# A fused attention and feed-forward kernel: 120 instead of 112 blocks of exponentials shared with VectorE

## The chip, the cores and the metric

The kernel runs on one core of a Trainium2 chip. TensorE (PE) multiplies matrices into PSUM, ScalarE (ACT) takes exponentials and other functions, VectorE (DVE) does elementwise work, GpSimd (POOL) small side work, and SyncE (SP) issues DMAs. The metric is device time in microseconds, the median of several runs. Before the change it is 861.0 us (three runs, 860.99 to 861.55).

## The reference

The input `A_x` has 2048 rows of 640. It is normalised; one branch is attention with 32 heads of 20, the other a feed-forward mixer, and the result joins them:

```python
xn = layernorm(x)                                   # 2048 x 640
q, k, v = split(xn @ wqkv)                          # 32 heads of 20
p = softmax(q @ k.T * 20 ** -0.5)                   # 32 x 2048 x 2048
s = concat(p @ v) @ wo
h = gelu(layernorm(xn) @ w1)                        # then four column groups shifted by rows
x1 = xn + shifted(h) @ w2
b = x1 + gelu(layernorm(x1) @ w3) @ w4              # inner width 1536
out = x + s * silu(b)
```

The attention has 32 x 2048 x 2048 = 134 million exponentials, by far the most of the elementwise work.

## The kernel before

**Tiling.** Heads are taken in 8 *quads* of 4. For each quad the queries are taken in 4 *groups* of 512, so there are 32 groups, written quad.group here and run one after the other (`attn_quad`, line 1184). In a group the 2048 keys are 16 *key tiles* of 128. For one key tile and four heads the scores are 128 x 2048; a *half* is two heads, 128 x 1024, and fills two PSUM banks.

**A plain key tile** (`score_act`, line 1378): TensorE computes the scores of each half either by rows (line 1375: four-row-group matmuls, the four heads at once) or by columns (line 1390); ScalarE takes one exponential of each half from PSUM to SBUF (`exp_act`, line 1432); then TensorE adds the weighted sum with the values, four matmuls at once (line 1233), into one PSUM bank that holds the group's output. Some key tiles score both halves in one step by rows, and a few take both halves in one wide exponential of 128 x 2048 (`score_rows`, lines 1398 to 1418). Which positions do so stands in the table `NR` (line 501): a number is a position in the group's list of plain tiles, 100 added means wide. Positions beyond the list have no effect.

**A shared block** (`score_both`, line 1438, and `block_bits`, line 1341) covers two key tiles. TensorE scores each of them by rows, all four heads in one step. ScalarE takes the exponential of one half of each tile. VectorE takes the other half: it turns the scores into 16-bit integers by one multiply and add out of PSUM (line 1459), which read as bfloat16 are a straight-line approximation of the exponential; three more copies with a constant added (line 1358) give the approximation at other offsets, and TensorE sums all four against weighted values (line 1367), so that the mean of the four is close to the exponential. For two of the four the values carry a factor, and these scaled values are made once by GpSimd (line 1179) for the key tiles 2, 3, 6, 7, 10, 11, 14, 15 that blocks use (`BLK`). The copies run over one block (2048 wide, a *single*) or over two (4096 wide, a *pair*). So a block has two exponentials on ScalarE where two plain tiles have four, and five weighted sums where two plain tiles have two.

**How many blocks a group has** is in the table `ND` (line 510), by quad and group, 0 to 4. `order` (line 520) builds the group's list of steps from it: with n blocks, 16 - 2n plain tiles are left, and `UNITS` (line 488) says at which positions the blocks stand, one block as a single, two as a pair, three as a pair and a single, four as two pairs. The last group of the last quad is built apart (`last_half`, line 1245) with two shared key tiles of its own. The table counts 112 blocks; its last entry, 4, is not used by that group, so 108 are run.

**Beside the attention** run, spread over the groups: the first normalisation, projections of values (first in group 0.0, then in quad 1) and of queries and keys for later heads (`stack`), the feed-forward branch (first layers in quads 0 and 1, normalisation and third and fourth layers in quads 2 to 6, with long Gelu instructions on ScalarE), and in the last quad the output projection, with the gate on VectorE. All of their matmuls go into three single PSUM banks (4, 5, 6) and are taken out mostly by VectorE.

**Buffers.** Seven PSUM banks serve scores and the other matmuls: a plain half takes banks 0, 1 or 2, 3; a shared tile takes one of these pairs and two of the banks 4, 5, 6, or both pairs. Where the two banks are not neighbours (4 and 6) VectorE's conversion is two instructions of 512. There are seven SBUF buffers for exponentials (`PT`), two for a pair's integers (`U`) and three for copies (`SS`).

**What sets the order.** No engine chooses anything at run time. `TABLE` (line 1812) is a long string; two characters name a task, and one more the PSUM banks or buffer that it gets. `follow` (line 217) reads it from left to right, and each engine's queue has its tasks in that order. `plan_sync` (line 304) then derives the semaphore waits from reads, writes and the reuse of buffers. Each queue is strictly in order, so a waiting instruction holds back all behind it on its engine.

**After a group** (`normalise`, line 1466) VectorE transposes the output in 32 x 32 blocks out of PSUM, takes the reciprocals of the sums, multiplies, transposes back, and SP stores the heads with four DMAs. Each group but 0.0 also loads a copy of its queries with four DMAs.

Of the kernel before, what the change touches and what calls it, by code (L numbers as in the profile page):

```python
# [453 lines left out]
class Cfg:  # L454
# [5 lines left out]
    def __init__(self, S=2048, D=640, H=32, F=1536):  # L460
# [50 lines left out]
            [0, 4, 4, 3],  # L511
            [4, 4, 4, 4],
            [3, 1, 4, 4],
            [4, 3, 4, 4],
            [3, 4, 4, 4],
            [4, 3, 4, 4],
            [3, 4, 4, 4],
            [4, 3, 2, 4])
# [56 lines left out]
class Gen:  # L575
# [29 lines left out]
    def A(self, name, *key):  # L605
        a = (name,) + key
        self.pl.own(name, a)
        return a
# [1324 lines left out]
```

## Time and profile before

| | us |
|---|---|
| median of three runs | 861.0 |
| the profiled execution's own time | 861.55 |
| its span, first to last instruction | 859.6 |
| ScalarE busy | 815.5 |
| PE busy | 800.6 |
| VectorE busy | 734.7 |
| 788 exponentials of 128 x 1024 (line 1432), busy | 733.1 |
| conversions on VectorE (line 1459), busy | 263.7 |
| shifted copies (line 1358), busy | 194.7 |

A profile line of a group reads: kernel line, engine, operation, output and input names, shapes, count, then the time in which the group was busy, the mean length of one in ns, the idle time of the engine just before its instructions and what ended most of that. Instructions of one engine overlap by a little, so the sum of lengths is above the time that they take. Matmuls are pipelined four at a time and their ends are modelled, so that a PE shown as busy may still take more work.

### The profile page before, as it was taken

How to read it: one execution, taken by the hardware profiler on the slowest of the kernel's cores; microseconds unless marked ns; L12 is line 12 of the kernel's file. 1: busy time of each engine (PE TensorE's matmuls, PEld its weight loads, DVE VectorE, ACT ScalarE, POOL GpSimd, SP SyncE). 2: the span in 40 equal slices, each digit the busy share in tenths (PEclk: the TensorE clock that was granted, in tenths of full speed). 3: DMA queues.
4: the chain of work that ended last, by engine and by line, in shares of the span. 5: the costliest groups of instructions: out<-in, count | busy, mean ns of one | idle time of the engine just before them, and what ended most of it. 6: DMA issues, size and time to landing. Idle time of an engine off the chain costs nothing.

```text
span 859.6 us, 31925 instructions
## 1 busy us (share of the span) xinstructions
PE 800.6 (93%) x14542; PEld 338.8 (39%) x14542; DVE 734.7 (85%) x1031; ACT 815.5 (95%) x854; POOL 39.3 (5%) x75
## 2 busy tenths in 40 slices
PE   7999999999899999999988999999997899989996
PEld 4443333334344433333433444343333343424464
DVE  7649999998998899999877999998995889987655
ACT  7799999999999999999999999999999999999994
POOL 5510000000000000000000000000000000000000
PEclk9999999999999999999999999999999999999998
DMA  7000533222110022311033011313211102041312
GB/s 230 18 16 24 137 97 89 90 66 65 25 40 16 18 50 55 79 44 46 11 94 92 14 51 27 81 36 89 50 32 47 34 13 54 13 123 33 116 57 95
DMA packets 74487, 50.83 MB, mean 59 GB/s; under 512 B 44768, under 2 KB 69552, under 8 KB 74352
## 3 DMA queue, kind: packets, MB, share of 16 engines
q1 hardware_dynamic: 74352, 48.79, 21.1%
q8 instruction: 115, 1.88, 0.9%
q14 instruction: 20, 0.16, 0.1%
HBM read 34.53 MB, written 10.17 MB: 52 GB/s over the span
## 4 chain that ended last, share of the span: by engine, by line
ACT 63%; PE 29%; DVE 7%; issue 1%; DMA 1%; SPq 0%; DVEq 0%
ACT arena L1432 57%; PE psum L640 10%; PE psum L1375 5%; PE psum L1390 4%; PE psum L1367 3%; PE psum L1233 3%; DVE arena L1459 2%; ACT arena L1787 2%; PE psum L1274 1%; ACT arena L1803 1%; DVE arena L1358 1%; ACT arena L1414 1%; ACT arena L1716 1%; DVE arena L852 1%; PE psum L963 1%
## 5 line engine op out<-in xcount | busy, mean ns | idle before, releaser
L1432 ACT ACTIVATE arena<-psum 128x1024 bf16<-128x1024 f32 x788 | 733.1, 1039 | 20.8 <-PE psum L1375 17.8
L640 PE MATMUL psum<-arena 128*32 128x320 bf16 (+1 forms) x5952 | 359.2, 335 | 0.6 <-DVE arena L1459 0.2
L1459 DVE TENSOR_SCALAR arena<-psum 128x1024 uint16<-128x1024 f32 (+1 forms) x243 | 263.7, 1094 | 31.8 <-PE psum L1375 30.5
L640 PEld LDWEIGHTS psum<-arena 128*32 128x32 bf16 x5952 | 148.8, 97 | 132.6 <-issue 31.2
L1375 PE MATMUL psum<-arena 32*128 32x512 bf16 x1384 | 165.6, 387 | 34.6 <-ACT arena L1432 24.2
L1358 DVE TENSOR_SCALAR arena<-arena 128x4096 uint16<-128x4096 uint16 (+1 forms) x174 | 194.7, 1142 | 2.9 <-PE psum L1367 1.8
L1390 PE MATMUL psum<-arena 128*32 128x512 bf16 x2400 | 182.7, 381 | 3.1 <-ACT arena L1432 2.1
L1233 PE MATMUL psum<-arena 128*22 128x512 bf16 x1552 | 148.9, 383 | 2.4 <-ACT arena L1432 2.0
L1367 PE MATMUL psum<-arena 128*22 128x512 bf16 x1728 | 146.2, 381 | 3.3 <-DVE arena L1358 3.1
L1375 PEld LDWEIGHTS psum<-arena 32*128 32x128 bf16 x1384 | 42.0, 91 | 179.5 <-ACT arena L1432 115.1
L1390 PEld LDWEIGHTS psum<-arena 128*32 128x32 bf16 x2400 | 46.1, 95 | 69.3 <-ACT arena L1432 57.7
L1367 PEld LDWEIGHTS psum<-arena 128*22 128x22 bf16 x1728 | 40.6, 91 | 53.6 <-issue 15.5
L1233 PEld LDWEIGHTS psum<-arena 128*22 128x22 bf16 x1552 | 38.8, 91 | 49.9 <-issue 18.6
L1109 DVE CAST arena<-psum 128x512 bf16<-128x512 f32 x40 | 27.0, 682 | 11.7 <-PE psum L640 11.4
L1783 DVE CAST arena<-psum 128x512 bf16<-128x512 f32 x48 | 32.7, 681 | 3.0 <-PE psum L640 2.5
L1567 DVE SCALAR_TENSOR_TENSOR arena<-psum,arena 128x320 bf16<-128x320 f32 x32 | 15.5, 489 | 22.5 <-PE psum L640 22.3
L1171 DVE CAST arena<-psum 128x320 bf16<-128x320 f32 x32 | 15.1, 486 | 16.2 <-PE psum L640 16.0
L852 DVE BATCH_NORM_STATS2 arena<-arena 128x6 f32<-128x320 bf16 x54 | 23.7, 477 | 3.2 <-DMA arena<-in_A_x_dram 3.1
L1480 DVE STREAM_TRANSPOSE arena<-psum 128x512 f32<-128x512 f32 x31 | 21.9, 708 | 1.7 <-PE psum L1367 1.2
L1490 DVE STREAM_TRANSPOSE arena<-arena 128x512 bf16<-128x512 bf16 x31 | 21.8, 702 | 0.2
L1744 DVE TENSOR_TENSOR arena<-psum,arena 128x320 bf16<-128x320 f32 x32 | 15.1, 480 | 7.2 <-PE psum L640 7.0
L1488 DVE TENSOR_TENSOR arena<-arena 128x512 bf16<-128x512 f32 x31 | 21.1, 680 | 0.1
(118 smaller groups left out, 364.2 us busy)
## 6 DMA issues: line engine op xcount, KB each, us to landing
arena<-in_B_w_dram SPq DMA_DIRECT2D x48, 160.0 KB, 2.6
arena<-arena SPq DMA_DIRECT2D x124, 32.0 KB, 2.2
arena<-in_B_w_dram SPq DMA_DIRECT2D x4, 960.0 KB, 5.7
arena<-in_A_x_dram SPq DMA_DIRECT2D x8, 320.0 KB, 5.9
arena<-in_A_x_dram SPq DMA_DIRECT2D x16, 160.0 KB, 2.3
out_dram<-arena SPq DMA_DIRECT2D x16, 160.0 KB, 1.8
heads<-arena SPq DMA_DIRECT2D x112, 20.0 KB
arena<-keys SPq DMA_DIRECT2D x28, 80.0 KB
```

The lines of the kernel that those rows point to most:

```text
L640: ins = e.matmul(pb[32 * c:32 * c + 32, 0:N], lhsT(k, c), rhs(k, c), start=(k == 0), stop=(stop and k == nk - 1), tile_position=(0, 32 * c))
L852: lambda e, li=li, n=n, hh=hh: e.bn_stats(st[:, li, 6 * hh:6 * hh + 6], xn[:, n, hD * hh:hD * hh + hD]),
L1109: T("dve", c_dve(512), lambda e, h=h, c=c: e.tensor_copy(KS[:, 512 * c:512 * c + 512], self.wbank(h)[:, 0:512]), reads=[wa], writes=[A("KS ...
L1233: ins = e.matmul(pb[32 * i:32 * i + 22, 0:512], VA[:, ql, kts[i // 2], i, :], PT[:, slots[i // 2][0].slot, 512 * (i % 2):512 * (i % 2) + 512],
L1358: T("dve", c_dve(w, "4x"), lambda e, v=v, dst=dst: e.tensor_scalar(dst, U[:, ub, 0:w], EXP_B[v], None, op0=ALU.add), reads=halves, writes= ...
L1367: ins = e.matmul(pb[32 * i:32 * i + 22, 0:512], wv, dst[:, at:at + 512].bitcast(BF16), start=first, stop=final, tile_position=(0, 32 * i))
L1375: return e.matmul(out, self.KT[32 * i:32 * i + 32, b, 128 * kt:128 * kt + 128], self.QT[32 * i:32 * i + 32, b, 512 * qc:512 * qc + 512], s ...
L1390: ins = e.matmul(out[32 * c:32 * c + 32, :], self.KT[:, b, 128 * kt + 32 * c:128 * kt + 32 * c + 32], self.QM[:, gb, 2 * a + jj, :], start ...
L1432: lambda e: e.activation(self.PT[:, hp.slot, :], self.psum[:, 512 * hs.slot:512 * hs.slot + 1024], AF.Exp, scale=cfg.scale),
L1459: ins = e.tensor_scalar(U[:, ub, 1024 * at + 512 * k:1024 * at + 512 * k + w], self.psum[:, 512 * hd.slots[k]:512 * hd.slots[k] + w], a_ex ...
L1480: T("dve", c_dve(512), lambda e: e.transpose(Ob[:, :], self.bank(self.PVB)[:, :]), writes=[("PV", 0), A("Ob")], name=f"ob{quad}_{qc}", cls ...
L1783: T("dve", c_dve(512), lambda e, h=h, fc=fc, i=i: e.tensor_copy(GT[:, i, fc, :], self.wbank(h)[:, 0:512]), reads=[wa], writes=at, name=f"g ...
```

## The change

Two things change: six entries of `ND`, and `TABLE`, whose every line differs. Quad 0 group 0 goes from 0 to 2 blocks, quad 2 group 1 from 1 to 3, quad 4 group 0 and quad 6 group 0 from 3 to 4, quad 7 group 1 from 3 to 4 and quad 7 group 2 from 2 to 3. The table counts 120 blocks, of which 116 are run. `NR`, `UNITS`, the buffers and all functions stay; because the list of plain tiles gets shorter, an entry of `NR` beyond its end loses its effect (a wide exponential at position 9 of quad 7 group 1, a row-scored tile at position 8 of quad 6 group 0).

```diff
         self.ND = (
-            [0, 4, 4, 3],
+            [2, 4, 4, 3],
             [4, 4, 4, 4],
-            [3, 1, 4, 4],
+            [3, 3, 4, 4],
             [4, 3, 4, 4],
-            [3, 4, 4, 4],
+            [4, 4, 4, 4],
             [4, 3, 4, 4],
-            [3, 4, 4, 4],
-            [4, 3, 2, 4])
+            [4, 4, 4, 4],
+            [4, 4, 3, 4])
...
 TABLE = (
...
```

The new `TABLE` is another order of all tasks on all engines, with its own choice of banks and buffers; it is an encoded string of some 12,800 characters, as before, and is not shown.

## The prediction

> **What bounds the kernel now.** I read the engine totals and the slices first, then the chain of waits, then the groups of instructions kept apart by shape, then the busy times cut at the ends of the 32 groups of queries, then who waited for whom.
>
> The page, sections 1, 2, 4 and 5:
>
> ```profile
> PE 800.6 (93%) x14542; PEld 338.8 (39%) x14542; DVE 734.7 (85%) x1031; ACT 815.5 (95%) x854; POOL 39.3 (5%) x75
> ...
> DVE  7649999998998899999877999998995889987655
> ACT  7799999999999999999999999999999999999994
> ...
> ACT 63%; PE 29%; DVE 7%; issue 1%; DMA 1%; SPq 0%; DVEq 0%
> ...
> L1432 ACT ACTIVATE arena<-psum 128x1024 bf16<-128x1024 f32 x788 | 733.1, 1039 | 20.8 <-PE psum L1375 17.8
> ```
>
> ScalarE is busy in 9 tenths or more of every slice between the first two and the last, and 788 exponentials idle for only 20.8 us in total. Everything removed from that queue is time, unless a new wait takes its place. VectorE is next, at 85%.
>
> The groups by shape, which price VectorE's share:
>
> ```profile
> L1459 DVE TENSOR_SCALAR arena<-psum 128x1024 uint16<-128x1024 f32 x189 | 229.2, 1213 | 26.1 <-PE psum L1375 24.9
> L1358 DVE TENSOR_SCALAR arena<-arena 128x4096 uint16<-128x4096 uint16 x150 | 179.0, 1216 | 0.9
> L1358 DVE TENSOR_SCALAR arena<-arena 128x2048 uint16<-128x2048 uint16 x24 | 15.7, 680 | 2.0 <-PE psum L1367 1.8
> ```
>
> The chain, and VectorE's timeline, give the real pace of back-to-back instructions: 41 exponentials in 37.85 us are 0.923 us each (not the 1.039 of one), and VectorE's starts lie 1.13 to 1.14 us apart (not 1.21):
>
> ```profile
> 381.44 37.85 ACT arena L1432 x41
> ```
>
> ```profile
> 300.74 1.21 DVE L1459 TENSOR_SCALAR arena<-psum 128x1024 uint16<-128x1024 f32 x1
> 301.88 1.21 DVE L1358 TENSOR_SCALAR arena<-arena 128x4096 uint16<-128x4096 uint16 x1
> 303.01 1.21 DVE L1459 TENSOR_SCALAR arena<-psum 128x1024 uint16<-128x1024 f32 x1
> ```
>
> The busy times between the last exponentials of neighbouring groups. The rows are quad 0 group 0; quad 2 groups 1, 2, 3; quad 4 group 0; quad 6 group 0; quad 7 groups 1 and 2 (columns: stretch, length, busy of PE, weight loads, DVE, ACT):
>
> ```profile
> 33.70:65.30 31.60, 31.59 (x518) 12.15 (x510) 13.46 (x24) 30.66 (x33) 13.43 (x14) 1.00 0.07 16
> ...
> 263.40:291.60 28.20, 27.83 (x616) 13.90 (x614) 21.54 (x49) 27.84 (x31) 1.11 (x2) 1.00 0.04 10
> 291.60:314.30 22.70, 20.39 (x324) 7.02 (x316) 22.69 (x36) 22.16 (x25) 1.78 (x2) 1.00 0.11 25
> 314.30:340.00 25.70, 23.96 (x372) 8.43 (x368) 25.70 (x34) 23.69 (x27) 0.00 (x0) 1.00 0.27 65
> ...
> 446.20:471.00 24.80, 22.06 (x408) 9.39 (x404) 19.09 (x28) 23.95 (x26) 0.34 (x1) 1.00 0.39 105
> ...
> 635.30:673.70 38.40, 31.29 (x482) 12.35 (x478) 25.12 (x33) 37.10 (x28) 0.00 (x0) 0.96 0.15 45
> ...
> 766.00:792.00 26.00, 23.45 (x412) 9.64 (x405) 20.11 (x27) 25.17 (x27) 0.00 (x0) 0.93 0.29 90
> 792.00:818.80 26.80, 25.36 (x518) 12.29 (x518) 17.49 (x28) 25.78 (x28) 0.00 (x0) 1.00 0.32 99
> ```
>
> Six of these eight stretches get the new blocks. VectorE idles in them for 18.1, 6.7, 5.7, 13.3, 5.9 and 9.3 us. The two that follow quad 2 group 1 have no idle time at all, yet ScalarE was still busy 22.16 of 22.70 and 23.69 of 25.70 us: a full VectorE has so far cost ScalarE 0.5 and 2.0 us a group.
>
> Who waits where ScalarE and VectorE meet:
>
> ```profile
> PEld psum L1375 <- DVE arena L1459: 40.6, 88, 1.6
> ...
> ACT arena L1432 <- PE psum L1375: 17.8, 35, 0.9
> ```
>
> **The change, part by part.** The table of shared blocks goes up by 2 in quad 0 group 0, 2 in quad 2 group 1, and 1 each in quad 4 group 0, quad 6 group 0, quad 7 groups 1 and 2: 8 blocks.
>
> *ScalarE loses.* A block is two key tiles; of their four half exponentials two go to VectorE, so 16 would go. In quad 7 group 1 the wide exponential stood at position 9 of ten plain tiles; with eight left it vanishes with its tile, so there the loss is one wide piece (1.77 us alone in the chain) and no narrow one. So 14 x 0.923 + 1.77 = 14.7 us. None of this lies beside longer work: it is the queue that bounds.
>
> *VectorE gains.* 16 conversions at 1.13 = 18.1 us. Shifted copies: the single units become 6 from 8 and the pairs 55 from 50, three copies each, so 15 more wide at 1.13 = 17.0, and 6 fewer narrow at 0.60 (0.680 less the same overlap) = 3.6. Together +31.5 us. The starts in the timeline show an instruction beginning some 0.08 us before the end of the one ahead. The Trainium skill (VectorE: DVE Perf Modes, The DRAIN you can't avoid) says that the next operation waits until the pipe has emptied; by the full lengths of the rows that would be 16 x 1.213 + 15 x 1.216 - 6 x 0.680 = 33.6 us, some 2 us more against this change. The spacing of the starts decides for 31.5. What covers it is VectorE's idle time, 81 us between 65.3 and 818.8 (753.5 us long, 672.2 busy in the sums of these stretches). Outside quad 0 group 0 the load is 31.5 - 7.9 = 23.6, and the cover shrinks by the 11.0 us that ScalarE saves there: 81 - 23.6 - 11.0 leaves about 46 us of 742, 6%.
>
> *TensorE.* Where plain scores run by columns, a block drops four halves at 0.44 (by the starts of its matmuls around 303 us, as the next prices) and two weighted sums at 0.22, and adds two four-way scores at 0.32 and five sums at 0.22: -1.76 + 0.64 + 0.66, about -0.5 us a block. In quad 0 group 0 scores already run by rows, at 0.31 a half: -1.24 + 0.64 + 0.66, nothing. Six blocks save 2.8 us on an engine beside the path: taken as 0, ends -2.8 and 0.
>
> *SP and POOL.* No DMA and no POOL instruction is added; every group loads its queries and stores its heads as before. Quad 0 group 0 now needs the scaled values of tiles 2, 3, 6, 7, which POOL made at 43 to 63 us, inside that group; the last was ready at 63.5, and a stretch shortened by 3.7 would end at 61.6. Cost 0, as sums may come in any order; ends 0 and 1.9, inside (a) below.
>
> *Three give-backs.* (a) Quad 0 group 0: 3.7 us of exponentials go, but PE is busy 31.59 of 31.60 there with value and query projections that the group itself needs. Ends 0 and 3.7; I take 1.8, half, since neither row decides. By matmul busy time PE is full and the 3.7 would be lost; the Trainium skill (Perfetto Trace Analysis, Identifying the Most-Contended Engine) calls that a poor measure and would look at weight loads, here 12.15 of 31.60, by which all 3.7 would be gained. (b) Quad 2: VectorE has 6.7 us idle, loses 3.7 of it and receives 7.9, so 4.9 us spill into two stretches without room. If the feed-forward work of those stretches is put off to quad 3, which idles, it costs 0; if not, 4.9. I take 2.5. (c) The whole order of instructions is new, and all semaphores with it. Groups idle ScalarE for 0.65 us on average (20.8 over 32) and 2.1 at worst (109.6 to 136.0). If the two worst fell to the mean, -2.8; if the six changed groups rose to the worst from their mean of 0.9, +7.2. I take +2.5, as these groups become like the full ones of quad 2.
>
> Sum: -14.7 + 1.8 + 2.5 + 2.5 = -7.9 us. The profiled execution took 861.55 (span 859.6 and 1.95 around it), which stands 0.55 above the median of 861.0: 853.6 for such an execution, 853 against the median.
>
> **The rivals.** *VectorE becomes the bound (slower).* Where VectorE has no room, a block does not shorten its stretch by 1.85 but lengthens it by 31.5/8 = 3.9 us. It decides from 14.7 = n x 5.8, so n = 2.5: with three of eight blocks on a full VectorE the time is 861.0 - 9.2 + 11.8 = 863.6, with four (both in quad 2, both in quad 0) 869. For it: 25.70 busy of 25.70 in quad 2, and PE's 40.6 us of waits for the conversions, which hold the banks. Against it: four of the blocks fall on stretches with 5.7 to 13.3 us idle and need 3.9 + 1.85 each.
>
> *Nothing given back.* All projections and feed-forward work move into the idle time: 861.0 - 14.7 = 846.3, and 843.5 if the two worst groups mend too. For it: full groups with under 1 us of ScalarE idle. Against: PE's row in quad 0.
>
> *The gain is hidden.* The order's waits eat it: with (a), (b), (c) at their bad ends -14.7 + 3.7 + 4.9 + 7.2 = +1.1, so 859 to 862. That ScalarE does not lose the pieces cannot be; the code emits them.
>
> **How the numbers follow.** My forecast, 848 to 858, has 0.53; nothing given back 0.09; hidden 0.12 (half of it still faster by 0.2%, most of the rest the same); VectorE as the bound 0.26, nearly all slower. 0.2% of 861 is 1.7 us, about what a measurement of this kernel can tell. So faster 0.66, same 0.07, slower 0.27. The range that leaves out two in ten goes from 845 to 866: under the full gain, over three blocks on a full VectorE. The forecast's own range is 848 to 858.
>
> **What would show it.** ScalarE: 774 narrow and 8 wide exponentials, busy near 800.8. VectorE: 165 wide and 18 narrow copies, busy near 766, about 90% of the span. (a) shows in the length from the first exponential to quad 0's first transposed sums, 31.6 now and 29.7 forecast; (b) in ScalarE's idle time in quad 2, 2.9 us now over these three stretches and 5.4 forecast; (c) in the idle time before the exponentials, 20.8 now. The prediction is wrong if that last number rises past 35, or if VectorE is the longest part of the chain.

## The result, and the profile after

The changed kernel takes 865.5 us (median of four runs, 863.5 to 866.8) where the kernel before, timed beside it, takes 861.2: a ratio of 1.0048, interval [1.0028, 1.0068]. It is slower by half a per cent, where a gain of 8 us was forecast. The profiled execution took 865.4 us, its span is 862.5.

The page of the kernel after, in its sections 1, 4 and 5:

```profile
PE 802.3 (93%) x14542; PEld 339.8 (39%) x14542; DVE 765.3 (89%) x1070; ACT 803.2 (93%) x839; POOL 42.7 (5%) x75
...
ACT 53%; PE 29%; DVE 16%; issue 1%; DMA 1%; SPq 0%; DVEq 0%
...
L1432 ACT ACTIVATE arena<-psum 128x1024 bf16<-128x1024 f32 x774 | 722.5, 1036 | 38.4 <-PE psum L1375 32.9
```

ScalarE did lose its exponentials, and its busy time fell by 12.3 us. The idle time just before exponentials rose from 20.8 to 38.4 us: more came in as idle time, 17.6 us, than went out as work. Of the 38.4 us, 32.9 end with a score of TensorE (line 1375).

The groups of instructions by shape, after:

```profile
L1459 DVE TENSOR_SCALAR arena<-psum 128x1024 uint16<-128x1024 f32 x191 | 232.0, 1215 | 25.7 <-PE psum L1375 24.0
L1358 DVE TENSOR_SCALAR arena<-arena 128x4096 uint16<-128x4096 uint16 x165 | 197.8, 1224 | 0.9
...
L1459 DVE TENSOR_SCALAR arena<-psum 128x512 uint16<-128x512 f32 x82 | 52.4, 680 | 4.1 <-PE psum L1375 3.9
```

Sixteen more conversions were due, but only 2 are whole ones; the other 14 came as 28 halves (82 from 54). A conversion falls in two halves where its tile's two banks are 4 and 6, not next to each other. This points at less choice of banks in the new order. Its table shows another sign of that: a tile shared by ScalarE and VectorE takes one pair of banks (0,1 or 2,3) and two of banks 4 to 6, or it takes both pairs. The table before has 8 such tiles, the table after 17: three more in group 0.0, four in 2.1, one each in 4.0, 7.1 and 7.2, and one less over the unchanged groups. (0.0 stands for quad 0 group 0.)

The waits between TensorE and the two engines that read its banks, after:

```profile
PEld psum L1375 <- DVE arena L1459: 44.3, 99, 1.6
...
ACT arena L1432 <- PE psum L1375: 32.9, 60, 2.2
```

ScalarE waited for scores 60 times where it had been 35, and the longest wait was 2.2 us, not 0.9.

The busy times between the last exponentials of neighbouring groups, after, for the same eight stretches as in the prediction (length, then busy time of PE, weight loads, VectorE, ScalarE and POOL, and the granted clock, which is the share of its full speed that TensorE was given):

```profile
33.30:65.50 32.20, 31.19 (x560) 13.15 (x556) 21.74 (x33) 26.84 (x29) 15.21 (x14) 1.00 0.07 16
...
264.40:293.30 28.90, 27.44 (x614) 13.94 (x606) 28.51 (x58) 24.59 (x27) 1.11 (x2) 1.00 0.03 8
293.30:316.10 22.80, 20.37 (x314) 7.03 (x306) 22.78 (x37) 22.27 (x25) 2.32 (x2) 1.00 0.11 26
316.10:341.60 25.50, 23.57 (x352) 8.38 (x348) 25.48 (x33) 23.69 (x26) 0.00 (x0) 1.00 0.27 67
447.90:472.80 24.90, 23.42 (x456) 10.42 (x448) 22.65 (x28) 22.76 (x25) 0.64 (x2) 1.00 0.39 107
636.90:676.60 39.70, 33.59 (x544) 13.49 (x540) 29.61 (x38) 35.54 (x26) 0.00 (x0) 0.91 0.15 41
...
768.50:797.10 28.60, 25.00 (x408) 10.36 (x408) 25.13 (x31) 24.04 (x27) 0.00 (x0) 0.88 0.19 58
797.10:823.70 26.60, 24.41 (x492) 11.60 (x484) 22.17 (x38) 24.38 (x26) 0.00 (x0) 1.00 0.29 87
```

Set beside the rows before, ScalarE is less busy in all six changed groups, and only 7.2 became shorter by more than 0.1 us. By the exact ends of the exponentials the lengths went from 31.67 to 32.05 us (0.0), 28.23 to 28.95 (2.1), 24.89 to 24.84 (4.0), 38.41 to 39.74 (6.0), 25.89 to 28.54 (7.1) and 26.90 to 26.62 (7.2): together +4.8 us, where -14.7 of exponentials had left them. The other groups changed by +0.3 us together, and the end of the kernel, behind the last exponential, became 2.2 us shorter (11.0 to 8.9). So nearly all of the loss stands in the groups that were to gain, and 4.0 us of it in 6.0 and 7.1.

Two of these stretches, 6.0 and 7.1, also have a lower clock than before (0.91 from 0.96, 0.88 from 0.93). In windows of 2 us at the start of 7.1, after:

```profile
770.00:772.00 2.00, 0.78 (x6) 0.20 (x6) 1.96 (x3) 2.00 (x3) 0.00 (x0) 1.00 0.04 9
772.00:774.00 2.00, 0.70 (x12) 0.21 (x12) 1.99 (x3) 1.60 (x3) 0.00 (x0) 1.00 0.91 305
774.00:776.00 2.00, 1.76 (x18) 0.32 (x10) 1.90 (x3) 1.94 (x3) 0.00 (x0) 0.52 0.19 49
776.00:778.00 2.00, 1.81 (x20) 0.63 (x20) 1.97 (x2) 2.00 (x3) 0.00 (x0) 0.50 0.00 0
778.00:780.00 2.00, 2.00 (x32) 0.96 (x28) 1.31 (x2) 1.10 (x2) 0.00 (x0) 0.50 0.04 8
```

TensorE was idle for over half of 4 us (770 to 774), and then ran at half clock for 6.83 us. ScalarE starves at the end of that piece (1.10 of 2.00). Before, the same group had 3.41 us at half clock.

### The profile page after: what moved, and what is told of

Its sections match the earlier page's. It is cut to its first block, busy times and chain, and to the rows that moved or that the text cites. A ratio compares the mean times of both kernels' runs of the same rounds, so it can differ in the third digit from the quotient of the medians.

```text
span 862.5 us, 31939 instructions
## 1 busy us (share of the span) xinstructions
PE 802.3 (93%) x14542; PEld 339.8 (39%) x14542; DVE 765.3 (89%) x1070; ACT 803.2 (93%) x839; POOL 42.7 (5%) x75
## 4 chain that ended last, share of the span: by engine, by line
ACT 53%; PE 29%; DVE 16%; issue 1%; DMA 1%; SPq 0%; DVEq 0%
ACT arena L1432 47%; PE psum L640 11%; DVE arena L1459 6%; PE psum L1375 5%; DVE arena L1358 4%; PE psum L1390 4%; PE psum L1367 3%; PE psum L1233 3%; ACT arena L1787 2%; DVE arena L852 2%; PE psum L1274 1%; ACT arena L1716 1%; ACT arena L1803 1%; DVE arena L1744 1%; DVE arena L1783 1%; ACT arena L1414 1%
## 5 line engine op out<-in xcount | busy, mean ns | idle before, releaser
L1432 ACT ACTIVATE arena<-psum 128x1024 bf16<-128x1024 f32 x774 | 722.5, 1036 | 38.4 <-PE psum L1375 32.9
L640 PE MATMUL psum<-arena 128*32 128x320 bf16 (+1 forms) x5952 | 363.8, 336 | 3.5 <-DVE arena L1171 2.0
L1459 DVE TENSOR_SCALAR arena<-psum 128x1024 uint16<-128x1024 f32 (+1 forms) x273 | 284.3, 1054 | 29.8 <-PE psum L1375 27.9
L1358 DVE TENSOR_SCALAR arena<-arena 128x4096 uint16<-128x4096 uint16 (+1 forms) x183 | 209.4, 1171 | 1.1
L1390 PE MATMUL psum<-arena 128*32 128x512 bf16 x2272 | 174.0, 382 | 1.0 <-ACT arena L1432 0.6
L1367 PE MATMUL psum<-arena 128*22 128x512 bf16 x1856 | 161.2, 380 | 2.7 <-DVE arena L1358 2.5
L1233 PE MATMUL psum<-arena 128*22 128x512 bf16 x1520 | 144.7, 383 | 1.3 <-ACT arena L1432 1.0
L1367 PEld LDWEIGHTS psum<-arena 128*22 128x22 bf16 x1856 | 44.1, 91 | 56.1 <-issue 16.3
L1233 PEld LDWEIGHTS psum<-arena 128*22 128x22 bf16 x1520 | 38.3, 92 | 50.2 <-issue 17.8
L1490 DVE STREAM_TRANSPOSE arena<-arena 128x512 bf16<-128x512 bf16 x31 | 21.7, 702 | 0.1
L1787 ACT ACTIVATE arena<-arena 128x12288 bf16<-128x12288 bf16 x2 | 20.9, 10445 | 0.0
```

The source lines that it names most:

```text
L640: ins = e.matmul(pb[32 * c:32 * c + 32, 0:N], lhsT(k, c), rhs(k, c), start=(k == 0), stop=(stop and k == nk - 1), tile_position=(0, 32 * c))
L1233: ins = e.matmul(pb[32 * i:32 * i + 22, 0:512], VA[:, ql, kts[i // 2], i, :], PT[:, slots[i // 2][0].slot, 512 * (i % 2):512 * (i % 2) + 512],
L1358: T("dve", c_dve(w, "4x"), lambda e, v=v, dst=dst: e.tensor_scalar(dst, U[:, ub, 0:w], EXP_B[v], None, op0=ALU.add), reads=halves, writes= ...
L1367: ins = e.matmul(pb[32 * i:32 * i + 22, 0:512], wv, dst[:, at:at + 512].bitcast(BF16), start=first, stop=final, tile_position=(0, 32 * i))
L1390: ins = e.matmul(out[32 * c:32 * c + 32, :], self.KT[:, b, 128 * kt + 32 * c:128 * kt + 32 * c + 32], self.QM[:, gb, 2 * a + jj, :], start ...
L1432: lambda e: e.activation(self.PT[:, hp.slot, :], self.psum[:, 512 * hs.slot:512 * hs.slot + 1024], AF.Exp, scale=cfg.scale),
```

## The experiments

Every ratio is to runs of the kernel before on the same chip. Lengths of groups are from one profile each, from last exponential to last exponential; a profiled execution can lie well off the median (e4's took 856.07 us where the median is 861.04, e8's 858.2 where it is 854.78). To relieve an engine means here to leave out part of its work.

**Which engine's relief is worth something (e1 to e4).** Theory S: ScalarE's relief is worth its price, and something that the change adds eats it. Theory O: the relief itself is not worth it. e1 is the kernel before with ScalarE's part of the change alone:

```diff
+CUT = {"0_0": (6, 7, 10, 11), "2_1": (6, 7, 10, 11), "4_0": (14, 15), "6_0": (14, 15), "7_1": (14, 15), "7_2": (10, 11)}
...
+        w = 64 if cut(tag) else 1024
-               lambda e: e.activation(self.PT[:, hp.slot, :], self.psum[:, 512 * hs.slot:512 * hs.slot + 1024], AF.Exp, scale=cfg.scale),
+               lambda e: e.activation(self.PT[:, hp.slot, 0:w], self.psum[:, 512 * hs.slot:512 * hs.slot + w], AF.Exp, scale=cfg.scale),
```

> The kernel before, with 15 narrow exponentials and one half of a wide one in the six groups that the change touches cut from 1024 to 64 columns (the weighted sums then read old values for the rest, so part of the exponentials is left out); nothing is added to VectorE or PE and the order is the one of before. Theory S (my prediction's: ScalarE sets the length of these six groups): about 0.8 us a piece, 12 to 13 us, so 848 to 850. Theory O (other engines set their length already, so ScalarE's pieces were nearly free there): under 4 us, 857 to 861, with the groups 0.0 and 2.1 hardly shorter. Each group's length from the trace tells them apart one by one.

It took 862.34 us, ratio 0.9994 [0.9984, 1.0004]: nothing. ScalarE's busy time fell by 11.0 us (804.5 from 815.5; the short pieces that are left keep some of it). The stretches 0.0 and 2.1 of e1:

```profile
35.30:67.00 31.70, 31.67 (x521) 12.21 (x518) 13.48 (x24) 27.96 (x33) 13.51 (x14) 1.00 0.07 16
265.00:293.10 28.10, 27.73 (x616) 14.35 (x614) 21.56 (x49) 25.04 (x31) 1.11 (x2) 1.00 0.04 11
```

ScalarE does 2.7 to 2.8 us less in each and both are as long as before. PE's columns stay at 31.67 of 31.70 and 27.73 of 28.10. The idle time before exponentials rose from 20.8 to 32.4 us: the relief was handed back as waits. Theory S falls here, before any of VectorE's new work is added.

e2 is the kernel after with VectorE's share of six of the new blocks (all but those of 0.0) cut to 64 columns:

```diff
+NEW = {"2_1": (1, 2), "4_0": (3,), "6_0": (3,), "7_1": (3,), "7_2": (2,)}
...
+            if is_new(quad, self_qc, kt // 4):
+                return e.tensor_scalar(U[:, ub, 1024 * at:1024 * at + 64], self.psum[:, 512 * lo:512 * lo + 64], a_exp, EXP_BIAS, op0=ALU.mult, op1=ALU.add)
```

> The changed kernel, with VectorE's conversions and copies for the new blocks of five groups (all but quad 0 group 0, 6 blocks) cut to 64 columns, or to the part that the kernel before had; part of the approximated exponentials is left out, order and waits stay. Theory V (the new blocks' load on VectorE gives the gain back): the five groups lose their ScalarE idle time, 10 to 12 us, so 853 to 856, quad 2 group 1 about 4 us shorter. Theory P (PE and its banks, through the other matmuls that share these groups): under 3 us, 862 to 865.

864.91 us, ratio 1.0033 [1.0019, 1.0047], so 1.3 us of the 4.1, and the intervals overlap: theory V falls. Group 2.1 stayed at 28.95 us although VectorE now idles for 6.45 us in it, where the kernel after left it 0.39. VectorE alone is not what holds that group.

e3 and e4 relieve TensorE, in the kernel after and the kernel before: the matrix products of the projections are cut to 64 columns after their first step.

```diff
+                w = 64 if k and name[:2] in ("v0", "v1", "w1", "w2", "w3", "w4", "wo", "s0", "s1") else N
...
-                    ins = e.matmul(pb[32 * c:32 * c + 32, 0:N], lhsT(k, c), rhs(k, c), start=(k == 0), stop=(stop and k == nk - 1),
+                    ins = e.matmul(pb[32 * c:32 * c + 32, 0:w], lhsT(k, c), rhs(k, c)[:, 0:w], start=(k == 0), stop=(stop and k == nk - 1),
```

> The changed kernel, with the matmuls of the value, query, key, feed-forward and output projections after the first step of each tile cut to 64 columns, so most of these products is left out; scores, weighted sums, evictions, order and waits stay. Theory P: the changed groups get the time that ScalarE saved, 10 us or more, so 850 to 855, and more than the kernel before gets from the same cut. Theory V: under 4 us, 861 to 865.

> The kernel before, with the same cut of the projections' matmuls as in the run on the changed kernel (most of these products is left out). If ScalarE bounds the kernel before as I read it, under 4 us, 857 to 861; if PE bounds some of its groups, quad 0 group 0 and quad 2 group 1 above all, 6 us or more, with these groups shorter.

863.01 us, ratio 1.0011 [0.9992, 1.003], and 861.04, ratio 0.9977 [0.9959, 0.9995]: by the ratios 3.2 us under the kernel after and 2.0 us under the kernel before. Neither reached what was expected if TensorE bounds these groups (10 us and 6 us). The totals are no clean measure of TensorE's load: its granted clock fell to 0.958 and 0.963 of full speed in the two profiles (0.986 and 0.988 in the two whole kernels) and to 0.944 in another run of e4, with pieces of up to 13.65 us at half clock. But in e4 no such piece lies in 0.0 or 2.1:

```profile
32.80:63.90 31.10, 26.84 (x519) 9.68 (x518) 13.98 (x24) 30.55 (x34) 13.52 (x14) 1.00 0.07 16
260.40:288.20 27.80, 25.75 (x614) 11.67 (x614) 21.19 (x48) 27.73 (x32) 1.11 (x2) 1.00 0.04 11
```

With 4.8 and 2.1 us less on TensorE they took 31.09 and 27.81 us, 0.6 and 0.4 less than before, and now ScalarE is the full engine, with 30.55 of 31.10 and 27.73 of 27.80 us. Under e1 it was TensorE. In e3 group 2.1 took 28.40 us at full clock, with VectorE busy for 27.84 of them.

**What a tile over both pairs costs (e5).** Eight shared tiles of the kernel before, in groups where ScalarE hardly idles, get both pairs. The edit is in the order table alone; decoded it reads:

```diff
-tile 7 of 3.2: banks 0,1 for ScalarE, 4,5 for VectorE
+tile 7 of 3.2: banks 0,1 for ScalarE, 2,3 for VectorE
...
```

> The kernel before with eight of its shared tiles (the seventh key tile of groups 1.1, 3.0, 3.2, 4.1, 4.2, 5.0, 6.1 and 6.2) given both of ScalarE's pairs of PSUM banks instead of one pair and two banks of 4 to 6; the same instructions otherwise, the whole computation. This makes 16 such placements where the kernel before has 8 and the changed one 17. Theory P (a tile over both pairs makes the next scores wait for a running exponential, so that ScalarE stands for one eviction-free stretch on each side): each costs 0.5 to 1.8 us, so +4 to +14 us over the kernel before, 866 to 876 us, with ScalarE's idle time before exponentials up from 20.8 us by about as much, in just these groups. Rival Q (the placement is free, the stalls of the changed kernel come of TensorE having more to do than it can in those groups): under +2 us, and lengths of these groups within 0.4 us of before.

874.58 us, ratio 1.0148 [1.013, 1.0166]: 11.9 us for eight tiles, 1.49 each. The groups with such a tile grew by 1.11 to 1.68 us, the others by 0.6 at most (6.0) and most of them by nothing. ScalarE in group 3.2, in the kernel before:

```profile
387.82 23.16 ACT L1432 ACTIVATE arena<-psum 128x1024 bf16<-128x1024 f32 x25
```

and in e5:

```profile
389.24 4.75 ACT L1432 ACTIVATE arena<-psum 128x1024 bf16<-128x1024 f32 x5
394.49 1.02 ACT L1432 ACTIVATE arena<-psum 128x1024 bf16<-128x1024 f32 x1 [0.50 <-PE psum L1375]
396.21 1.02 ACT L1432 ACTIVATE arena<-psum 128x1024 bf16<-128x1024 f32 x1 [0.69 <-PE psum L1375]
397.41 16.66 ACT L1432 ACTIVATE arena<-psum 128x1024 bf16<-128x1024 f32 x18 [0.18 <-PE psum L1390]
```

One unbroken row of 25 exponentials becomes rows of 5, 1, 1 and 18 with 0.50, 0.69 and 0.18 us between them, 1.37 in all. The scores need a free pair while the other is being read; with both pairs in one tile there is none. TensorE, in e5, at the second gap:

```profile
395.78 0.39 PE L1375 MATMUL psum<-arena 32*128 32x512 bf16 x2 [1.33 <-DVE arena L1459]
```

Its next score waited 1.33 us for VectorE's conversion, and ScalarE waited for the score. So theory P stands, in groups where ScalarE sets the pace, and Q falls. A block saves ScalarE 1.84 us (14.7 over 8), and one such tile in it takes 1.49 back there.

**Both reliefs together (e6).** The edits of e1 and e4 in one kernel.

> The kernel before with both reliefs at once: 16 exponentials of the six changed groups cut to 64 columns (as in e1) and the matrix products of the recurrent projections after their first step cut to 64 columns (as in e4); the output is left wrong in both parts. If ScalarE and TensorE are both full in groups 0.0 and 2.1, so that neither relief alone could shorten them, the two together do: 0.0 at 28.5 to 30 us (31.1 with TensorE's alone, 31.7 with ScalarE's alone) and 2.1 at 25.5 to 27 us (27.8 and 28.1), and the total 6 us or more below e4. Rival (a chain of waits through the banks and tiles, not the load of an engine, sets the pace): both within 0.5 us of e4, and the total within 2 us of it.

857.76 us, ratio 0.9946 [0.9931, 0.9961], 2.7 us under e4 by the ratios, at a clock of 0.952. Group 0.0 took 30.49 us and 2.1 27.23, each 0.6 us less than in e4. The theory of two full engines said 1.1 and 0.8 us or more, and 6 us or more in all; its rival, a chain of waits, at most 0.5, 0.5 and 2. The result lies between them, nearer the rival. The two groups, both at full clock:

```profile
33.00:63.50 30.50, 26.80 (x518) 9.78 (x510) 13.95 (x24) 27.92 (x34) 13.43 (x14) 1.00 0.07 16
262.90:290.20 27.30, 25.37 (x614) 11.57 (x614) 21.16 (x48) 25.10 (x32) 1.11 (x2) 1.00 0.04 11
```

No engine is full here: the busiest one idles for 2.6 and 1.9 us. So in this order the two full engines of 0.0 and 2.1 have waits between engines close behind them, only 1.2 and 1.0 us under the groups' lengths before. Which waits they are was not traced.

**Is it the order, the number of blocks, or their place (e7 to e12)?** I searched new order tables for the kernel with 112 blocks, with 120, and with parts of the change: e10 has the blocks of 4.0, 6.0, 7.1 and 7.2, e11 those of 0.0 and 2.1, e12 those of 6.0 and 7.2 alone. e7 and e9 are edits of `TABLE` alone, the others of `ND` too, as in the change; none leaves work out. e7 and e8 were timed on one chip, e9 to e12 on another, so across the two the ratios compare. For e12:

```diff
-            [3, 4, 4, 4],
-            [4, 3, 2, 4])
+            [4, 4, 4, 4],
+            [4, 3, 3, 4])
...
 TABLE = (
...
```

> The 112 blocks of the kernel before, the same instructions, with an order table that I searched anew; 7 tiles lie over both pairs. Theory O (it is the order and the banks that it hands out, not the number of shared blocks, that holds the time): the kernel before gains 4 to 10 us by a new table alone, 851 to 857 us, and lies within 3 us of the 120 blocks ordered by the same search (e8). Rival R (120 blocks are worth their 14.7 us of ScalarE once ordered well; only the changed kernel's table is poor): this one gains less than 2 us over the kernel before, and e8 lies 6 us or more below it.

> The 120 blocks of the changed kernel, the same instructions, with an order table searched in the same way; 16 tiles lie over both pairs. Theory O: within 3 us of e7, 851 to 858 us. Rival R: 6 us or more below e7, at 850 us or less. If placements over both pairs are dear whatever the order (theory P of e5), this one is 5 us or more above e7.

> 112 blocks as before, the order of e7 searched on for longer; 7 tiles over both pairs. It is the base X for the next three, which are ordered by the same search. Expected 850 to 853 us, at or under e7's 852.4.

> 116 blocks: of the eight that the change adds, only the four in groups 4.0, 6.0, 7.1 and 7.2 (one each); ordered by the same search; 9 tiles over both pairs, two more than e9. Theory B (a block saves 14.7/8 = 1.84 us of ScalarE, and each tile over both pairs gives 1.4 us back, e8's 31.9 us of idle time less e7's 19.3 over nine more such tiles): -7.4 + 2.8 = 4.6 us below e9. Rival C (nothing that is taken from ScalarE reaches the end, since another engine or a chain of waits is as long): within 1.5 us of e9.

> 116 blocks: the other four of the eight, two in group 0.0 and two in 2.1, where projection tiles hold banks 4 to 6; same search; 14 tiles over both pairs, seven more than e9. Theory B: -7.4 + 7 x 1.4 = +2.4 us against e9, and 7.0 us above e10, which has the same ScalarE work. Rival A (ScalarE's work alone counts): the same as e10, 7.4 us below e9. Rival C: within 1.5 us of both.

> 114 blocks: only the two in groups 6.0 and 7.2, which got no more tiles over both pairs in e8 than in e7; same search; 7 tiles over both pairs, as many as e9. Theory B: 2 x 1.84 = 3.7 us below e9. Rival C: within 1.5 us of e9. Should B hold, this or e10 is the fastest kernel of the case, at 846 to 849 us.

| | blocks | tiles over both pairs | us | ratio and interval | idle before exponentials, us |
|---|---|---|---|---|---|
| e7 | 112 | 7 | 852.38 | 0.9886 [0.9866, 0.9906] | 19.3 |
| e8 | 120 | 16 | 854.78 | 0.9914 [0.9884, 0.9944] | 31.9 |
| e9 | 112 | 7 | 850.56 | 0.9864 [0.984, 0.9887] | 16.2 |
| e10 | 116 | 9 | 850.92 | 0.9861 [0.984, 0.9883] | 22.6 |
| e11 | 116 | 14 | 854.36 | 0.99 [0.9882, 0.9918] | 24.9 |
| e12 | 114 | 7 | 852.89 | 0.9874 [0.9852, 0.9897] | 21.7 |

A new order alone is worth 10 to 12 us to the kernel before, and it is the fastest of the case, level with e10. No kernel with more blocks is clearly below e9 in the orders that this search found: theory O. The 120 blocks were not searched as long as e9. e8 is 2.4 us over e7, within theory O's 3 us and short of the 5 that its nine more tiles over both pairs were to cost if dear in any order. In the profiled executions e8's first exponential begins 3.9 us later than e7's (34.32 and 30.39 us), and from there to the last one the two take 813.6 and 812.6 us. Rival A falls: e11 and e10 have the same ScalarE work and lie 3.4 us apart. Rival C has e10 within its 1.5 us of e9, but e11 3.8 us above. Theory B, a price for each block and each tile over both pairs, got the sign of e11 against e10 right (3.4 us for five more such tiles, where it said 7.0) and failed on the gain: e10 was to be 4.6 us under e9 and is level, e12 3.7 under it and is 2.3 over it (0.9 by the ratios, whose intervals overlap).

Where the gain of e10 went can be read group by group. The stretches 6.0, 7.1 and 7.2 of e9:

```profile
625.80:665.60 39.80, 33.84 (x538) 12.63 (x534) 29.22 (x41) 37.10 (x29) 0.00 (x0) 0.91 0.10 27
757.30:782.30 25.00, 21.68 (x362) 8.57 (x358) 22.47 (x31) 24.98 (x27) 0.00 (x0) 1.00 0.30 99
782.30:809.20 26.90, 25.17 (x492) 11.59 (x490) 17.88 (x28) 26.00 (x28) 0.00 (x0) 1.00 0.27 81
```

and of e10:

```profile
627.70:665.30 37.60, 32.84 (x541) 13.49 (x538) 30.80 (x38) 35.60 (x26) 0.00 (x0) 0.95 0.20 54
758.10:785.70 27.60, 24.18 (x410) 10.50 (x406) 24.71 (x34) 23.68 (x26) 0.00 (x0) 0.94 0.39 119
785.70:811.30 25.60, 24.84 (x500) 12.07 (x496) 23.54 (x38) 24.30 (x26) 0.00 (x0) 1.00 0.25 71
```

6.0 and 7.2, whose new tiles found banks 4 to 6, are 2.1 and 1.3 us shorter (6.0 in part because its piece at half clock is 3.41 us and not 6.83). 7.1, with a tile over both pairs and a piece at half clock that e9 does not have, is 2.7 us longer, and 4.0, with one such tile, 0.6. So a block can pay in its own group. In e12, where only 6.0 and 7.2 have blocks, they are 2.2 and 0.4 us shorter, and 7.1, unchanged in its blocks, is 2.3 us longer with 6.83 us at half clock.

**Is TensorE the second bound (e13 to e15)?** e13 was to issue every weighted sum over ScalarE's tiles twice in the six groups; e14 is e9 with the relief of e1.

> The kernel before with every weighted sum over ScalarE's tiles issued twice in the six changed groups (84 instructions of four matrix products, 0.215 us each by the starts: 3.4 us in group 0.0, 3.2 in 2.1, 2.8 each in 4.0, 6.0 and 7.1, 3.0 in 7.2, 18.1 in all; sums and values both come out wrong there). Theory T (TensorE is as full as ScalarE in 0.0 and 2.1, and partly in the others): by PE's busy row the slack is 0.0 us in 0.0, 0.4 in 2.1, 2.6 in 4.0, 7.1 in 6.0, 2.5 in 7.1, 1.4 in 7.2, so 0.0 grows by 3 to 3.5 us, 2.1 by 2.5 to 3, the others by 0 to 1.6, in all +7 to +11 us over the kernel before. Rival (ScalarE alone sets the pace and a busy TensorE still has room, since its matrix products overlap): 0.0 and 2.1 grow by under 1 us each, in all under +3 us.

> The reordered 112 blocks of e9 with the same 16 exponentials as in e1 cut to 64 columns (14.7 us of ScalarE; the rest of these tiles is left unwritten). Rival V (e1 gained nothing only because the table before was made for ScalarE's old pace): 5 us or more below e9, so a ratio to the kernel before of 0.981 or less. Theory T (another engine is as full, whatever the order): under 2.5 us below e9, a ratio of 0.9835 to 0.988, and ScalarE's idle time before exponentials up from 16.2 us to 25 us or more.

e13 missed: the function that issues the sums read the group's number after the loop over the groups had ended, so nothing was added (1552 matrix products of that line, as before). It says nothing on TensorE; it is the kernel before once more, at a ratio of 0.9993 [0.9981, 1.0005]. Its profile shows what two executions of the same instructions differ by: 0.0 and 2.1 within 0.01 us, but 4.0 0.76 us longer, with a 3.41 us piece at half clock that the other execution did not have, and 6.0 0.39.

e14 took 853.26 us, ratio 0.9893 [0.9877, 0.991]: no gain on e9, rather a loss of 2.5 us by the ratios, whose intervals just overlap, and a little outside theory T's range. Groups 0.0 and 2.1 took 31.64 and 27.52 us (31.64 and 27.64 in e9), and the idle time before exponentials rose to 28.0. Rival V falls: a better order does not let the relief through.

e15 is e13 with the sums issued:

```diff
...
+                m = 2 if f"{quad}_{qc}" in TWICE else 1
-                def fnpv(e, kts=kts, slots=slots, ends=ends):
+                def fnpv(e, kts=kts, slots=slots, ends=ends, m=m):
...
-                    for i in range(4):
+                    for i in range(4 * m):
+                        again, i = divmod(i, 4)
...
```

> The kernel before with the weighted sums over ScalarE's tiles in the six changed groups issued twice, as e13 meant to: 84 instructions of four matrix products, 0.215 us each by the starts: 3.4 us in group 0.0, 3.2 in 2.1, 2.8 each in 4.0, 6.0 and 7.1, 3.0 in 7.2, 18.1 in all. Theory T (TensorE is full in 0.0 and 2.1): with the slack that PE's busy row shows there (0.0 us and 0.4) 0.0 grows by 3 to 3.5 us and 2.1 by 2.5 to 3, the other four by 0 to 1.6 each, +7 to +11 us in all. Rival (a chain of waits, with room on TensorE): 0.0 and 2.1 grow by under 1 us each, under +3 us in all.

874.33 us, ratio 1.0131 [1.0111, 1.0151]: 11.8 us for 18.1 us of added sums, a little over theory T's range. The stretches 0.0, 2.1 and 7.2 of e15:

```profile
33.80:68.50 34.70, 34.70 (x581) 13.59 (x578) 13.14 (x24) 31.78 (x33) 13.50 (x14) 1.00 0.06 14
266.70:297.60 30.90, 30.78 (x672) 16.21 (x670) 21.85 (x49) 29.04 (x32) 1.11 (x2) 1.00 0.04 10
802.40:831.50 29.10, 28.44 (x586) 14.02 (x578) 17.84 (x28) 26.67 (x27) 0.00 (x0) 1.00 0.30 92
```

0.0 grew by 3.03 us (3.4 added), 2.1 by 2.62 (3.2), 7.2 by 2.22 (3.0, where at most 1.6 was expected); 7.1 and 4.0 by 1.0 and 0.9 against e13 (2.8 added to each), 6.0 not at all against it. The other groups grew by 1.6 us together. In the first three, holding five of the eight new blocks, TensorE's work is time: theory T stands there, and the rival of a chain of waits with room on TensorE falls.

In 4.0, 6.0 and 7.1 TensorE had room for most of the added work, and yet ScalarE's relief was worth nothing there either. Against e13, e1 took 25.61 us in 4.0 (25.65), 62.09 in 6.0 and 6.1 together (62.11), and 75.96 from 7.0 to 7.2 (75.87): what 6.0 and 7.1 gain alone, 0.8 and 1.2 us, the groups next to them lose.

## Why the prediction was wrong

**The step that failed** is "None of this lies beside longer work: it is the queue that bounds." ScalarE's queue bounds the span as a whole, and it was read from the span: 95%, every slice full, 20.8 us of idleness. Its pieces were priced as if nothing else in the six groups were as long, and they turned out to be worth nothing: with 11.0 us of ScalarE's work gone and nothing added the kernel took the same time (e1). So the term -14.7 came to about 0. In 0.0, 2.1 and 7.2 the longer work is TensorE's: of 9.6 us added to it there, 7.9 were added to the time (e15), and with TensorE relieved instead ScalarE is the full one in 0.0 and 2.1 (e4). In 4.0, 6.0 and 7.1, with three of the eight blocks, what stands beside ScalarE's queue was not found. Nor are the two engines all of it: with both relieved, waits keep 0.0 and 2.1 within 1.2 and 1.0 us of their length (e6). The rows for 0.0 and 2.1 stood in the prediction, PE 31.59 of 31.60 and 27.83 of 28.20; the rule was applied to 0.0 alone, at half weight, and 2.1 was overlooked. The prediction's own sign of being wrong, idle time before the exponentials past 35 us, came: it is 38.4.

**VectorE's cost** was right as a total: +30.6 us of busy time measured for +31.5, with 165 wide and 18 narrow copies. So was ScalarE's count: 774 and 8 exponentials, 803.2 us busy where 800.8 was forecast. VectorE's sum did not price that 14 conversions would come in halves, two of 0.68 us for one of 1.21.

**TensorE at 0** was right as a sum (802.3 from 800.6) and wrong as "an engine beside the path".

**Give-back (a)**, 1.8 of 3.7 us in 0.0: all 3.7 came back and 0.4 more; the length is 32.05 us (31.67 before) and not 29.7. Between two ways to read TensorE the half was taken, since "neither row decides". The matmul row decides here. The Trainium skill (Perfetto Trace Analysis, Identifying the Most-Contended Engine) advises against that row as a measure of how close TensorE is to its roofline. In this kernel, with its four matrix products at a time, the row at 31.59 of 31.60 meant that more work is more time, as e15's 3.03 of 3.4 us shows.

**Give-back (b)**, quad 2: ScalarE's idle time over the three stretches became 6.7 us where 5.4 was forecast: a fair size by luck, as it did not come from the spill that was forecast. Nothing spilled into 2.2 and 2.3, which took 22.74 and 25.48 us (22.74 and 25.70 before). It is all in 2.1 (0.40 to 4.31 us). VectorE has no room there, as forecast (28.51 of 28.90 us), but its relief changes nothing (e2), and TensorE's brings 0.55 us (e3). TensorE is busy for 27.44 us there, and four tiles lie over both pairs; the parts of these were not separated.

**Give-back (c)**, +2.5 for the new order, was the smallest look at the largest unknown. A mechanism was not seen: banks. The choice of banks is in the table's code and in `kind("SD", ...)`, and before's VectorE rows count 27 conversions in halves; the prediction read these only as prices. A tile over both pairs costs 1.49 us where ScalarE sets the pace (e5), and there are nine more of them. That price was not measured in the kernel after itself. Seven of the ten in changed groups fall on 0.0 and 2.1, where ScalarE has 3.7 us of room each after the relief, so they may cost less there. Two runs have the same seven tiles: e11 takes 33.64 and 28.74 us in these groups where e9 has 31.64 and 27.64, but 3.41 us of its 0.0 are at half clock; e8 takes 30.23 and 28.62 where e7 has 31.89 and 28.04, with 0.0 beginning later. So 2.1 gained nothing by its blocks in any of them, and for 0.0 it is open. In 6.0 and 7.1 the piece at half clock is twice as long as in the profile before.

**The rivals.** VectorE as the bound named the sign and not the cause: its relief in the changed kernel gives 1.3 us back, within the noise, and leaves 2.1 as long (e2), and it is 16% of the chain. "The gain is hidden" was nearest: the bad ends of (a), (b) and (c) made +1.1, and +4.3 was measured. It had been given 0.12. The prediction treated (a), (b) and (c) as three separate mishaps; (a) and 2.1's share have one cause in common, a TensorE as full as ScalarE in the groups before.

**What stays open.** What holds 4.0, 6.0 and 7.1 when ScalarE is relieved, and which waits stand behind the two full engines in 0.0 and 2.1. How the growth of 6.0 and 7.1 (1.3 and 2.7 us) divides between tiles over both pairs, the half clock and the order was not separated, and these two groups hold 4.0 of the 4.8 us. Why TensorE stands idle at the start of 7.1 in the kernel after was not traced. Kernel after with its new tiles kept on banks 4 to 6 was not tried.

## What to carry to other kernels

Before work is moved off the busiest engine, read the second busiest in the very stretches where it is moved, not over the span: where two engines are full the relief of one is worth next to nothing, and one run with the relief alone (e1) says so before the rest is built. A block of work has a price in buffers as well as in engine time; count who holds the banks where it goes. When a schedule is fixed in a table, compare a change with the old work under an equally searched table: here the order was worth 12 us and, in the orders found, the blocks nothing.

## What the hardware showed that was not expected

- In the kernel after, TensorE was busy for 0.78 and 0.70 us of two windows of 2 us, and then its granted clock stood at 0.5 for 6.83 us. In all profiles such pieces between the first and the last exponential last 3.41 us or a multiple of it (6.83, 10.24, 13.65). The same kernel has them at other places in another execution; one of 3.41 us came with 0.76 us more in group 4.0 (e13 against the first profile).
- Less work for TensorE came with a lower clock: with the projections cut its mean was 0.944 to 0.963 in ten runs (0.988 in the profile before), and the time fell by only 0.2% (e4). How much the clock took of the gain was not separated.
- In group 0.0 of the kernel after two wide shifted copies on VectorE took 3.90 us together, beside a memset on POOL that took 2.22 us; the mean copy takes 1.22, and the same memset took 1.29 in the kernel before. It was seen once and not tested.
